# Turning the last batch's x on VectorE and by SBUF transfers, a shorter head sort, and a re-planned order, in an attention and maxout kernel

## The chip, the cores and the metric

The kernel runs on one core of one Trainium2 chip. The metric is the device time of one execution in microseconds. Before the change the median of three runs is 190.68 us (189.26 to 191.23).

## The reference

```python
scores = scale * np.matmul(q, k.transpose(0, 1, 3, 2))      # B 4, H 8, S 768, D 64
stream_keep = causal & (is_sink | in_win)                   # 4 sinks, window 64
mask = np.where(retrieval_head, causal, stream_keep)        # is_retrieval = [1,0,1,0,0,0,1,0]
a = softmax(np.where(mask, scores, -1e9))
x = np.matmul(a, v).transpose(0, 2, 1, 3).reshape(B * S, H * D)
h1, h2 = x @ w1, x @ w2                                      # 512 x 1024 each
out = np.maximum(h1, h2) @ w_out                             # 1024 x 512, float32
```

## The kernel before, in words

**Heads.** Before anything else `head_order` (L1329) reads the eight flags and ranks the heads with ten small VectorE instructions on one partition: three heads with full causal attention ("F") come first, then five streaming heads ("S"), and a count. `values_load_multi_w_load_instructions` (L1413) loads the result into registers of every engine, and a branch (L1419) picks `tile_paired_heads` if the count is three. Only what needs no head number can be issued ahead of the branch: the mask table and two quarters of `moe_w2` (L1407).

**Attention.** A batch is four pairs of heads in the slots FF, FS, SS, SS; pair n of the program is batch n // 4, slot n % 4, so there are 16. A pair's q, k and v are loaded by SP's queue, cast to bf16 (L316, shared by all copies of VectorE and GpSimd; L314 is ScalarE's), and q and k are turned so that the head dimension lies on partitions: for n < 8 on TensorE (`turn`, tile pt, L405) with a copy from PSUM (`unturn`), after that by VectorE's 32x32 squares (`turn_squares`, L418) from a load that already placed the blocks (L349). Then for each tile of up to 8 blocks of 128x128: `scores` (tile ps, L480, with mask products L453 in the first batch), `exp` on ScalarE (tile at, L497), a mask product on VectorE (L519, from the second batch on), `weighted` (tile po, L541), and per half (three blocks of 128 tokens) `normalise` (reciprocal L556, two products L558), which writes the batch's x, 768 tokens x 512 features.

**x turned.** The second stage needs x with features on partitions (tile xt). `turn_x` (tile px, L574) does this on TensorE in 24 transposes of 128x128 a batch, 12 for each half, and `take_x` copies px to xt on VectorE or ScalarE in four copies a batch.

**Maxout.** max(x w1, x w2) w_out is computed as relu(x (w1 - w2)) w_out + x (w2 w_out). `up` (ph, L590) makes one of 8 column blocks for one half (384 tokens) in 4 matmuls, `relu` is on ScalarE (L601) or VectorE (L603), `down` (pout, L617) gives 128 tokens in 12 matmuls of 512 columns, `take_out` copies it and `store` (L655) sends it; the last 128 tokens are split in two column halves (L632, L644). w1 - w2 (`subtract`, L721), the bf16 w2, its turned form (`turn_w2`, pw, L676; `take_w2`) and w2 w_out (`product`, po2, L690) are made during the first batch and the start of the second. w1 and w_out come through the four buffers of q and k loads ("qn"), so their loads wait for casts.

**Order.** Everything after the branch is recorded as operations with a cost, dependences and a rank; `Order.run` (L118) plays it as a schedule with one clock per engine and emits the instructions in that order, so each engine's instruction stream is fixed when the program is built. TensorE takes from lists in the order TX (turn_x), W (weighted), S, TQ, F (up, down), P (weights), and D (`warm`, L729), products nobody reads, at most up to the planned time 20. The outputs of all but the scores share four PSUM banks, given out by the plan. The costs, the time at which the engines begin, and the time until which TensorE is planned at half rate (`order.warm`) are constants in the code.

Of the kernel before, what the change touches and what calls it, by code (L numbers as in the profile page):

```python
# [68 lines left out]
WARM = 60  # L69
# [14 lines left out]
class Order:  # L84
# [6 lines left out]
    def __init__(self, banks):  # L91
        self.ops, self.lists, self.banks = [], {}, banks
        self.users, self.bank, self.queue = [None] * banks, None, None
        self.warm = 0.0
# [23 lines left out]
    def run(self, names, together=(), spare=(), until=0.0, begin=None):  # L118
        free = dict.fromkeys(("PE", "SP", "DMA", "ACT", "DVE", "POOL"), 0.0)
        free.update(begin or {})  # L120
        waiting, pending = [], []
        at = {n: 0 for n in names}
        for k, o in enumerate(self.ops):
            o.number = k
            o.left = sum(d.end is None for d in o.deps) + (o.behind is not None)
            for d in o.deps:
                d.users.append(o)
            if o.behind is not None:
                o.behind.followers.append(o)

# [15 lines left out]
        def free_bank():  # L146

            able = [
                (0.0 if u is None else u.end + u.tail, k)
                for k, u in enumerate(self.users) if u is None or u.end is not None  # L150
            ]
            return min(able) if able else None
# [34 lines left out]
        while True:  # L187
            while waiting and waiting[0][0] <= t:
                pending.append(heapq.heappop(waiting)[2])
            times = [waiting[0][0]] if waiting else []  # L190
            done = False
            for e in ("ACT", "DVE", "POOL", "SP"):
                able = [o for o in pending if e in o.cost or (o.engine == "DMA" and o.by == e)]
                if not able:
                    continue
                if free[e] > t:
                    times.append(free[e])
                    continue
                for o in sorted(able, key=lambda o: (o.rank, o.ready, o.number)):
                    if o.engine == "DMA":  # L200
                        free[e] = t + o.issue
                        start = max(free[e], free["DMA"])
                        free["DMA"] = start + o.cost["DMA"]
                        end = free["DMA"] + 1.6
                    else:
                        end = t + o.cost[e]
                        if any(max(free[x], t) + c < end for x, c in o.cost.items() if x != e):
                            continue
                        free[e] = end
                    pending.remove(o)  # L210
                    o.emit(e)
                    release(o.followers, t)
                    finish(o, end)
                    done = True
                    break
            if free["PE"] <= t:
                best = pick()
                if best and best[1] <= t:
                    n = best[0]
                    now = t  # L220
                    for k in range(2 if n in together and not self.lists[n][at[n]].single else 1):
                        mine = self.lists[n][at[n]:at[n] + 1]
                        w = when(mine[0]) if mine else None
                        if w is None or w > now + 0.3:
                            break
                        o = mine[0]
                        at[n] += 1
                        if o.bank:
                            self.bank = free_bank()[1]
                            self.users[self.bank] = o.bank  # L230
                        o.emit("PE")
                        now += o.cost["PE"] * (2 if now < self.warm else 1)
                        finish(o, now)
                    free["PE"] = now
                    done = True
                elif best:
                    times.append(best[1])
            else:
                times.append(free["PE"])
            if done:  # L240
                continue
            later = [x for x in times if x > t]
            if not later:
                break
            t = min(later)
        for n in spare:
            for o in self.lists.get(n, ())[at[n]:]:
                o.end = t
        left = sum(o.end is None for o in self.ops)
        assert not left, f"{left} operations were not reached"  # L250
        return t


def tile_paired_heads(tc, q, k, v, w1, w2, w2f, wo, out, tab, heads):
# [12 lines left out]
    TURNED, ANY_CASTS = 2 * HP, HP  # L267
# [7 lines left out]
    atp, xp = pool("atp", SLOTS_OF["at"]), pool("xp", SLOTS_OF["x"])  # L275
    gp, small, outp = pool("gp", 2), pool("small", 3), pool("outp", SLOTS_OF["ot"])
# [11 lines left out]
    idle = keep.tile([128, 512], BF16, name="idle")  # L288
    nc.gpsimd.memset(idle, 0.0)
# [286 lines left out]

    def take_x(b, blocks):
        i, m = blocks[0], len(blocks)
        return lambda e: copy(
            e, xts[b % len(xts)][:, i:i + m].rearrange("f i k c -> f i (k c)"), T["px", b, blocks][:, 0:m]  # L580
        )
# [150 lines left out]
    sorted_ = order.given(5.0)  # L732
# [12 lines left out]
    def prepare_w12(half, rank):  # L745
        for two in range(2):
# [7 lines left out]
            for c in range(2):  # L754
                subs[half, two, c] = op(
                    None, {"DVE": 0.68, "POOL": 1.45}, subtract(half, two, c), [o, loaded], rank=rank
                )
                frees.append(subs[half, two, c])

    w2_left = [order.given(3.6 + 1.6 * two) for two in range(2)]  # L760
    for two in range(2):
        prepare_w2(0, two, w2_left[two], -1)

    def prepare_qk(n):
# [24 lines left out]
        if "S" in SLOTS[n % HP]:  # L789
            cost = {"DVE": 0.8 if n < HP else 0.5, "POOL": 1.1}  # L790
# [3 lines left out]
    def prepare_v(n):  # L794
# [6 lines left out]
        if "S" in SLOTS[n % HP]:  # L801
            cost = 0.5 if SLOTS[n % HP] == "FS" else 0.75
# [4 lines left out]
    def attend(n):  # L807
        biased = n < HP
        for t in tiles_of[n]:
# [3 lines left out]
            if biased:  # L813
# [8 lines left out]
                op("DVE", 0.13 + part[1] * part[2] / 1700, mask(n, t, *part), [e], rank=n)  # L822
# [4 lines left out]
        for half in range(2):  # L827
# [3 lines left out]
            norm = op("DVE", 1.0, normalise(n, half), [*done_with["x", b][0]], rank=n)  # L831
# [12 lines left out]
            if p == HP - 1:  # L844
# [13 lines left out]
    for n in range(HP):  # L858
        attend(n)
    prepare_w12(0, HP - 0.7)  # L860
# [61 lines left out]
    for _ in range(WARM):  # L922
        pe("D", 0.43, warm, bank=order.given(0.0))

    order.warm = 8.4
    order.run(
        ("TX", "W", "S", "TQ", "F", "P", "D"), together=("S",), spare=("D",), until=20.0,
        begin={"DMA": 5.8, "SP": 4.6, "DVE": 5.4, "ACT": 4.8, "POOL": 5.0, "PE": 4.7},
# [4 lines left out]
def tile_any_heads(tc, q, k, v, moe_w1, moe_w2, w2f, moe_w_out, out, is_retrieval, n_sink, window):  # L933
# [271 lines left out]

    load_w(moe_w2[:, 512:1024], w2f[:, :, 512:1024])
# [122 lines left out]
def head_order(nc, small, is_retrieval, H):  # L1329


    raw = small.tile([1, 2 * H], I32, name="raw")
# [3 lines left out]
    number = small.tile([1, H], F32, name="number")  # L1336
    for h in range(H):
        nc.vector.memset(number[:, h:h + 1], float(h))
    flag = small.tile([1, 2 * H], F32, name="flag")
    r = small.tile([1, H], F32, name="r1")  # L1340
    key = small.tile([1, H], F32, name="key")
    table = small.tile([1, H, H], F32, name="table")
    rank = small.tile([1, H], F32, name="rank")
# [3 lines left out]
    vec.tensor_single_scalar(out=flag, in_=raw, scalar=0.0, op=ALU.not_equal)  # L1347
    two = flag.rearrange("p (h two) -> p h two", two=2)
    vec.tensor_tensor(out=r, in0=two[:, :, 0], in1=two[:, :, 1], op=ALU.max)
    vec.tensor_reduce(out=found[:, H:H + 1], in_=r, op=ALU.add, axis=AX.X)  # L1350
    vec.scalar_tensor_tensor(
        out=key, in0=r, scalar=-float(H), in1=number, op0=ALU.mult, op1=ALU.add
    )
    by_row = lambda a: a.unsqueeze(2).to_broadcast([1, H, H])
    by_col = lambda a: a.unsqueeze(1).to_broadcast([1, H, H])
    vec.tensor_tensor(out=table, in0=by_col(key), in1=by_row(key), op=ALU.is_lt)
    vec.tensor_reduce(out=rank, in_=table, op=ALU.add, axis=AX.X)
    vec.tensor_tensor(out=table, in0=by_col(rank), in1=by_row(number), op=ALU.is_equal)
    vec.tensor_tensor(out=table, in0=table, in1=by_col(number), op=ALU.mult)
    vec.tensor_reduce(out=found[:, 0:H], in_=table, op=ALU.add, axis=AX.X)  # L1360
    vec.tensor_single_scalar(out=found_i, in_=found, scalar=float(H - 1), op=ALU.min)
# [4 lines left out]
def kernel(  # L1366
# [36 lines left out]

    found = head_order(nc, consts, is_retrieval, H)
    nc.scalar.dma_start(out=tab, in_=table_dram.ap())
    for two in range(2):
        nc.sync.dma_start(  # L1407
            out=w2f[:, 2 * two:2 * two + 2, 0:512],
            in_=moe_w2[256 * two:256 * two + 256, 0:512].rearrange("(c p) f -> p c f", p=128),
        )  # L1410
# [7 lines left out]
    if window <= 64 and n_sink <= 64:  # L1418
        with tc.If(count == N_FULL) as cmp:  # L1419
            tile_paired_heads(tc, *both, tab, heads)  # L1420
# [44 lines left out]
```

## Time and profile before

| | |
|---|---|
| median of three runs | 190.68 us |
| the profiled execution | 190.68 us |
| its span, first to last instruction | 188.6 us |
| outside the span | 2.1 us |
| TensorE busy | 173.3 us, 1706 matmuls |
| VectorE, ScalarE, GpSimd busy | 106.5, 113.7, 61.5 us |
| HBM read, written | 25.43 MB, 6.29 MB |

Times below are counted from the start of the span. A profile gives each instruction's start and duration per engine, and what released it; matmuls overlap in the array, so a group of 128-column transposes that lists 0.5 us each can start one every 56 ns. "Landing" is when a transfer's last packet has arrived and its semaphore says so. An instruction on SP's queue is an issue: it takes a third to half a microsecond there, and the bytes move afterwards on 16 DMA engines.

### The profile page before, as it was taken

To read this page: it belongs to the slowest core of one execution; us is meant where nothing else is said; L and a number is where in the kernel's file an instruction comes from. 1 tells how busy PE (TensorE), PEld (TensorE's weight loads), DVE (VectorE), ACT (ScalarE), POOL (GpSimd) and SP (SyncE) were. 2 spreads that over 40 slices of the span, in tenths; PEclk is the share of its full clock that TensorE was granted. 3 is DMA by queue.
4 is the path that set the end of the run, shared out by engine and by line. 5 is a ranking of instruction groups with operands and counts; after the bars stand their busy time and mean duration, and the time that the engine had idled before them with its cause. 6 is when DMAs were issued, how large, how long until landed. Compare 5 with 4: busy or idle time off the path is not lost.

```text
span 188.6 us, 4670 instructions
## 1 busy us (share of the span) xinstructions
PE 173.3 (92%) x1706; PEld 101.4 (54%) x1706; DVE 106.5 (56%) x249; ACT 113.7 (60%) x167; POOL 61.5 (33%) x82
## 2 busy tenths in 40 slices
PE   0699997999999999999999998899999999999990
PEld 0456654666566556655655465445564545545560
DVE  4547869861599799989998779863740000000000
ACT  3079786778779687747964869275732714625420
POOL 0405496405787345263751526342000000000000
PEclk9999999999999999999999999999999999999998
DMA  5899999899997999999999999833002112012022
GB/s 178 271 303 315 213 287 366 275 299 320 298 286 125 152 153 152 184 169 207 154 200 157 185 191 189 220 150 118 2 30 84 56 57 89 23 59 111 0 107 75
DMA packets 86914, 32.11 MB, mean 170 GB/s; under 512 B 76387, under 2 KB 80739, under 8 KB 86883
## 3 DMA queue, kind: packets, MB, share of 16 engines
q1 hardware_dynamic: 86594, 31.34, 71.3%
q10 hardware_dynamic: 288, 0.39, 0.7%
q8 instruction: 15, 0.25, 0.6%
q14 instruction: 17, 0.13, 0.3%
HBM read 25.43 MB, written 6.29 MB: 168 GB/s over the span
## 4 chain that ended last, share of the span: by engine, by line
PE 74%; DVE 11%; DMA 5%; ACT 3%; issue 2%; POOL 2%; POOLq 1%; ACTq 0%; SPq 0%; DVEq 0%
PE pout L617 28%; PE ph L590 21%; PE po L541 7%; PE ps L480 6%; DVE at L519 5%; DMA w2f<-in_moe_w_dram 4%; PE pt L405 3%; PE po L690 3%; PE px L574 2%; DVE x L558 2%; ACT at L497 2%; PE pout L632 1%; DVE qk L418 1%; PE pw L676 1%; POOL w2b L316 1%
## 5 line engine op out<-in xcount | busy, mean ns | idle before, releaser
L497 ACT ACTIVATE at<-ps 128x1024 bf16<-128x1024 f32 (+3 forms) x68 | 59.4, 917 | 18.4 <-PE ps L480 17.9
L590 PE MATMUL ph<-xt,w 128*128 128x384 bf16 x256 | 44.8, 326 | 1.0 <-DVE g L603 0.8
L617 PE MATMUL pout<-wob,g 128*128 128x512 bf16 x184 | 45.1, 379 | 0.0
L316 POOL CAST qb<-qn 128x768 bf16<-128x768 f32 x26 | 22.8, 880 | 39.4 <-DMA qn<-in_k_dram 20.4
L590 PEld LDWEIGHTS <-w 128*128 128x128 bf16 x256 | 24.1, 98 | 17.3 <-issue 1.0
L601 ACT ACTIVATE g<-ph 128x384 bf16<-128x384 f32 x54 | 26.5, 492 | 9.0 <-PE ph L590 8.8
L519 DVE TENSOR_TENSOR at<-at,tab 128x1024 bf16<-128x1024 bf16 (+5 forms) x45 | 27.8, 644 | 4.6 <-ACT at L497 4.4
L314 ACT COPY ot<-pout 128x512 f32<-128x512 f32 (+1 forms) x22 | 12.7, 577 | 28.2 <-PE pout L617 26.2
L617 PEld LDWEIGHTS <-g 128*128 128x128 bf16 x184 | 16.8, 98 | 18.0
L316 DVE COPY ot<-pout 128x512 f32<-128x512 f32 (+1 forms) x3 | 1.8, 596 | 42.8 <-PE pout L632 42.3
L541 PEld LDWEIGHTS <-at 128*128 128x128 bf16 x472 | 19.8, 98 | 10.9 <-DVE at L519 2.9
L541 PE MATMUL po<-vb,at 128*128 128x65 bf16 x372 | 23.4, 194 | 2.1 <-DVE at L519 1.3
L558 DVE TENSOR_TENSOR x<-po,rez 128x192 f32 x64 | 22.9, 357 | 2.2
L617 PE MATMUL pout<-w2o,xt 128*128 128x512 bf16 x92 | 23.6, 379 | 0.0
L480 PE MATMUL ps<-qk 64*128 64x128 bf16 (+2 forms) x292 | 21.4, 234 | 0.0
L316 POOL CAST vb<-vn 128x768 bf16<-128x768 f32 x16 | 13.6, 850 | 17.1 <-DMA vn<-in_v_dram 14.5
L480 PEld LDWEIGHTS <-qk 64*128 64x128 bf16 x292 | 11.9, 94 | 11.0 <-issue 8.0
L316 POOL COPY vx<-vb 64x650 bf16<-64x650 bf16 (+1 forms) x24 | 17.1, 714 | 1.4
L418 DVE STREAM_TRANSPOSE qk<-qb 128x768 bf16<-128x768 bf16 x16 | 15.4, 965 | 0.0
L617 PEld LDWEIGHTS <-xt 128*128 128x128 bf16 x92 | 8.3, 98 | 8.5 <-issue 0.2
L541 PE MATMUL po<-vx,at 128*128 128x65 bf16 x100 | 10.8, 194 | 0.0
L480 PE MATMUL ps<-qk,kx 64*128 64x128 bf16 x100 | 9.7, 216 | 0.0
(57 smaller groups left out, 139.3 us busy)
## 6 DMA issues: line engine op xcount, KB each, us to landing
vn<-in_v_dram SPq DMA_DIRECT2D x32, 192.0 KB, 4.3
out_dram<-ot SPq DMA_DIRECT2D x23, 256.0 KB, 3.1
qn<-in_q_dram SPq DMA_DIRECT2D x16, 192.0 KB, 4.1
qn<-in_k_dram SPq DMA_DIRECT2D x16, 192.0 KB, 3.9
qn<-in_q_dram SPq DMA_DIRECT2D x32, 96.0 KB, 4.1
qn<-in_k_dram SPq DMA_DIRECT2D x32, 96.0 KB, 3.4
w2f<-in_moe_w_dram SPq DMA_DIRECT2D x4, 512.0 KB, 6.9
w1f<-in_moe_w_dram SPq DMA_DIRECT2D x4, 512.0 KB, 5.9
```

The lines of the kernel that those rows point to most:

```text
L314: nc.scalar.copy(out=out, in_=in_)
L316: eng[e].tensor_copy(out=out, in_=in_)
L405: nc.tensor.transpose(pt[:, i:i + 128], T["qb", n][:, t, i:i + 128], ident)
L418: nc.vector.transpose(T["qk", n][:, t], T["qb", n][:, t])
L480: nc.tensor.matmul(ps[:, bank, e * 128:(e + m) * 128], lhsT=lhsT, rhs=qk[rows, 0, i * 128:(i + m) * 128], start=bank not in begun, stop=Tr ...
L497: nc.scalar.activation(out=at[:, 0:len(w), 0:w[0]], in_=T["ps", n, t][:, 0:len(w), 0:w[0]], func=ACT.Exp, scale=scale,)
L519: eng[e].tensor_tensor(out=at, in0=at, in1=tbl, op=ALU.mult)
L541: nc.tensor.matmul(po[:, hh, b[-1] - 3 * half, :], lhsT=at[:, bank, e * 128:(e + 1) * 128], rhs=rhs, start=first and (bank, hh, e, b) == m ...
L558: nc.vector.tensor_tensor(out=T["x", b][:, 3 * half:3 * half + 3, bass.ds(heads[2 * p + hh], 1), :], in0=po[:, hh, :, 0:D].unsqueeze(2), i ...
L590: nc.tensor.matmul(ph, lhsT=w12[:, kc, fc * 128:(fc + 1) * 128], rhs=xts[b % len(xts)][:, 3 * tg:3 * tg + 3, kc, :], start=(kc == 0), stop ...
L601: nc.scalar.activation(out=g[:, fc, :], in_=ph, func=ACT.Relu)
L617: nc.tensor.matmul(pout, lhsT=lhsT, rhs=rhs, start=(e == 0), stop=(e == len(steps) - 1))
```

## The change

1. `head_order` uses five VectorE instructions in place of ten: a code 2 + h/8 plus the flag, one `max` over the eight codes, which gives them sorted, a sum, and one shift-and-mask that takes head numbers and count out of the float's bits. Within each class the heads now come in falling order.
2. The zero tile `idle` is set before the branch, and six products of it (`FIRST`) run on TensorE ahead of the branch.
3. One quarter of `moe_w2` is loaded ahead of the branch in place of two; the other is loaded after the first batch's q, k and v, and its cast, its turn and the copy of that are planned with a later rank.
4. For the last batch, `turn_x` and `take_x` go. For each half, `turn_x_squares` turns 128 x 1536 elements in 32x32 squares on VectorE into a new tile xs, and 16 transfers from SBUF to SBUF (`regroup_x`, issued by SP, 24 KB each, runs of 64 B) place the squares in xt. They are queued between the stores.
5. Several planned costs, the begin times and `order.warm` are other constants. `vary` adds small random shifts to the ranks of some operations off TensorE, from 24 seeds written in the code. `run` is split into `plan` and emission.

```diff
@@ Order
+    def vary(self, seeds):
+        self.link()
+        movable = [o for o in self.ops if o.engine != "PE"]
+        for seed in seeds:
+            rng = random.Random(seed)
+            for o in rng.sample(movable, rng.choice((1, 2, 4, 8, 20))):
+                o.shift = o.shift + rng.gauss(0, 2.0) if rng.random() < 0.8 else 0.0
...
-                for o in sorted(able, key=lambda o: (o.rank, o.ready, o.number)):
+                for o in sorted(able, key=lambda o: (o.rank + o.shift, o.ready, o.number)):
@@ tile_paired_heads
+    def turn_x_squares(b, half):
+        def emit(_):
+            if half == 0:
+                T["xs", b] = xs_pool.tile([128, NB, d_model], BF16, tag="xs", name="xs")
+            rows = slice(3 * half, 3 * half + 3)
+            nc.vector.transpose(
+                T["xs", b][:, rows].rearrange("p i f -> p (i f)"),
+                T["x", b][:, rows].rearrange("p i h d -> p (i h d)"),
+            )
+        return emit
+    def regroup_x(b, half, g, a):
+        def emit(e):
+            rows = slice(3 * half, 3 * half + 3)
+            src = T["xs", b][32 * g:32 * g + 32, rows].rearrange(
+                "r i (k a s) -> r i k a s", k=KC, a=4
+            )
+            dma[e].dma_start(
+                out=xts[b % len(xts)][32 * a:32 * a + 32, rows, :, 32 * g:32 * g + 32],
+                in_=src[:, :, :, a],
+            )
+        return emit
...
-                    None, {"DVE": 0.68, "POOL": 1.45}, subtract(half, two, c), [o, loaded], rank=rank
+                    None, {"DVE": 0.85, "POOL": 1.3}, subtract(half, two, c), [o, loaded], rank=rank
...
-    w2_left = [order.given(3.6 + 1.6 * two) for two in range(2)]
-    for two in range(2):
-        prepare_w2(0, two, w2_left[two], -1)
+    w2_left = [order.given(4.0)]
+    prepare_w2(0, 0, w2_left[0], -1)
...
-                op("DVE", 0.13 + part[1] * part[2] / 1700, mask(n, t, *part), [e], rank=n)
+                op("DVE", 0.27 + part[1] * part[2] / 1850, mask(n, t, *part), [e], rank=n)
...
-            if p == HP - 1:
+            if p == HP - 1 and b >= SQUARES_FROM:
+                o = op("DVE", 2.0, turn_x_squares(b, half), norms[b, half], rank=n)
+                done_with["x", b][1].append(o)
+                x_ready[b, half] += [
+                    op("DMA", 0.4, regroup_x(b, half, g, a), [o, *done_with["xt", b][0]], rank=n)
+                    for g in range(4) for a in range(4)
+                ]
+            elif p == HP - 1:
...
+    w2_left.append(load(1.6, load_w2(0, 1)))
+    prepare_w2(0, 1, w2_left[1], HP - 0.7)
...
-    order.warm = 8.4
+    order.warm = 7.2
+    order.vary(SEEDS)
     order.run(
...
-        begin={"DMA": 5.8, "SP": 4.6, "DVE": 5.4, "ACT": 4.8, "POOL": 5.0, "PE": 4.7},
+        begin={"DMA": 4.2, "SP": 3.4, "DVE": 4.2, "ACT": 3.6, "POOL": 4.2, "PE": 3.5},
@@ head_order
+        nc.vector.memset(number[:, h], 2 + h / 8)
...
     vec.scalar_tensor_tensor(
+        out=coded, in0=raw.rearrange("p (h two) -> p h two", two=2), scalar=0.0, in1=number,
+        op0=ALU.not_equal, op1=ALU.add,
     )
+    vec.tensor_tensor(out=code, in0=coded[:, :, 0], in1=coded[:, :, 1], op=ALU.max)
+    vec.max(out=found[:, 0:H], in_=code)
+    vec.tensor_reduce(out=found[:, H:H + 1], in_=code, op=ALU.add, axis=AX.X)
+    vec.tensor_scalar(
+        out=found_i, in0=found.bitcast(I32), scalar1=19, scalar2=H - 1,
+        op0=ALU.logical_shift_right, op1=ALU.bitwise_and,
+    )
@@ the kernel, ahead of the branch
     found = head_order(nc, consts, is_retrieval, H)
+    nc.gpsimd.memset(idle, 0.0)
+    with tc.tile_pool(name="first", bufs=1, space=PSUM) as first:
+        unused = first.tile([128, 512], F32, name="unused")
+        for _ in range(FIRST):
+            nc.tensor.matmul(unused, lhsT=idle[:, 0:128], rhs=idle, start=True, stop=True)
     nc.scalar.dma_start(out=tab, in_=table_dram.ap())
-    for two in range(2):
-        nc.sync.dma_start(
-            out=w2f[:, 2 * two:2 * two + 2, 0:512],
...
+    nc.sync.dma_start(
+        out=w2f[:, 0:2, 0:512], in_=moe_w2[0:256, 0:512].rearrange("(c p) f -> p c f", p=128)
+    )
```

## The prediction

> **What bounds the kernel now.** First the page's shares and its slices.
>
> ```profile
> span 188.6 us, 4670 instructions
> PE 173.3 (92%) x1706; PEld 101.4 (54%) x1706; DVE 106.5 (56%) x249; ACT 113.7 (60%) x167; POOL 61.5 (33%) x82
> PE   0699997999999999999999998899999999999990
> DMA  5899999899997999999999999833002112012022
> ```
>
> TensorE is full from about 35 us to 184; the DMA engines are full until about 123. Then the stages (engines in the order PE, PEld, DVE, ACT, POOL; then granted clock, DMA share, GB/s):
>
> ```profile
> 13.00:24.00 11.00, 10.69 (x165) 6.88 (x162) 8.34 (x20) 9.64 (x12) 4.85 (x7) 1.00 1.07 260
> 24.00:35.00 11.00, 9.25 (x145) 5.62 (x143) 8.37 (x23) 8.18 (x12) 8.88 (x10) 1.00 1.00 341
> 47.00:140.00 93.00, 90.68 (x1039) 53.97 (x1038) 76.26 (x171) 63.91 (x89) 42.57 (x53) 1.00 0.90 167
> 140.00:185.00 45.00, 44.30 (x244) 23.40 (x240) 1.11 (x2) 18.78 (x37) 0.00 (x0) 1.00 0.18 68
> ```
>
> From 140 us on TensorE alone works, on maxout that was left over. So a wait in the attention costs only what TensorE then stands idle: what counts is TensorE's work, its gaps, and when its stream begins. Third, the chain of waits (start, length):
>
> ```profile
> 0.76 1.20 DMA raw<-in_is_retrieval_dram
> 1.98 0.17 DVE flag L1347
> ...
> 3.84 0.16 DVE found_i L1361
> 4.04 1.01 POOLq L1413
> ...
> 23.35 8.29 DMA w2f<-in_moe_w_dram
> 31.70 1.05 POOL w2b L316
> 32.79 0.63 PE pw L676 x8
> 33.45 1.01 ACT w2t L314
> 34.46 0.50 ACT xt L314
> 35.00 9.98 PE ph L590 x60
> ...
> 136.93 0.67 PE px L574 x12
> ...
> 139.50 0.67 PE px L574 x12
> ```
>
> The sort is on it, a weight load and the turn of weights are on it just before ph, and both px groups of the last batch. Last, VectorE's casts of the first q and k, which wait for their landing:
>
> ```profile
> 10.26 0.56 DVE L316 CAST qb<-qn 128x768 bf16<-128x768 f32 x1 [0.47 <-DMA qn<-in_k_dram]
> 11.63 0.56 DVE L316 CAST qb<-qn 128x768 bf16<-128x768 f32 x1 [0.82 <-DMA qn<-in_q_dram]
> 12.85 0.56 DVE L316 CAST qb<-qn 128x768 bf16<-128x768 f32 x1 [0.65 <-DMA qn<-in_k_dram]
> ```
>
> **Part 1, the sort.** Ten instructions run from 1.98 to 4.00. Five remain: coded and code take the steps of flag and r (0.19 and 0.20 from start to start), the sum that of L1350 (0.07), found_i 0.16; `max` over eight has no row, between 0.15 (a reduction over eight) and 0.25 (a table step); I take 0.24, nearest to steps that wait for the one before. Sum 0.86 to 0.96, so the result stands 1.1 us earlier, and so do the register loads (1.01 us) and every engine's start: first q issue 5.31 to 4.2.
>
> **Part 2, loads and first tiles.** The trace has the two w2f quarters landing at 5.21 and 7.12, then the first pair's q at 8.63 and 9.14, k at 10.16, and the second pair's k at 12.75: one stream, 0.5 to 0.7 us for 192 KB. With one quarter out of the way (1.9 us) and issues at 4.2, the stream moves by 1.1 (issues only) to 2.2 (issue step 0.52 from a first landing at 6.7, which is 4.2 plus the mask table's 2.7 from issue to landing). On VectorE one cast (0.72) and one copy (0.69) of weights leave the start. I take 1.9: the first scores, at 13.02 now, begin at 11.1.
>
> This stage is paced by ScalarE (9.64 of 11) and by arriving q, k, v, and both move. But the moved quarter now stands between the last v (landing 25.15) and w1f: the w1f quarters, landing at 27.42 and 28.77, come 1.35 (spacing of these two) to 1.9 later in the stream, and so where they were. Their subtractions, three of four now on GpSimd (1.27 each), end near 31.5. The last normalise of batch 0, now to 33.26, moves to 31.4; px and the copy to xt (0.7 each) follow, and the turn of weights that stood on the chain from 31.70 is, in the built order, behind the 64 ph matmuls. So ph begins at 33.1 in place of 35.0; lower bound for this gain 1.2, upper 2.2. The second half of ph needs GpSimd's last subtraction at 38.3; landing near 36 plus 1.27 gives 37.3, so no wait, but a bound of 0.5. Behind ph stands one weight turn more than before (8 matmuls, 0.45), which used to lie under the normalise. Front: 1.9 - 0.45 = **1.45**, between 0.3 and 2.2.
>
> The six early products fill TensorE while it waits for heads; they cost nothing, as 4.0 (start 1.4, six at 0.43) is before the branch at 4.2. They may open the clock earlier: 512 columns took 0.44 at 10.67 and 256 took 0.21 at 13.02, half rate, but 128-column transposes at 14.68 start every 56 ns. The rate changed near 13.5, 7.6 us after the first product at 5.87. The same distance from 1.4 gives 9.0, before the scores; worth 0.3 at most, kept for the range. The Trainium skill ("TensorE: Matmul & The Clock Gate", Part 1) says about 3.4 us of sustained work opens the gate, in a free-running window. By that the dummies alone would open it by 8.2, and the sum would be the same or 0.3 lower; no row here shows a run of 3.4 us without gaps at half rate.
>
> **Part 3, px.** 24 transposes leave TensorE: 0.67 twice in the chain, **1.34**. Four copies leave VectorE and ScalarE (0.69 and 0.59 each half). VectorE gets two turns of 1536 elements; 768 take 0.966 (L418), so 1.93 each. In the built order the first stands ahead of the last normalise and holds one PSUM bank 1.9 us longer, with nothing but pout behind it, which ScalarE copies; no cost.
>
> Cover: in today's times the last po ends at 137.8, the first turn 138.3, the second 141.2. ph of the last batch's first half is 1.34 earlier than now, at 157.0, the second at 170.0. SP's queue, in order, has after the batch's first store (140.2) four transfers, a store (142.8), three, a store (145.4), fourteen, a store, three, a store, four, a store, four; each waits for the one eight issues earlier too. At 0.52 from issue to issue (k loads: 0.32 at least, and 0.19 between) the sixteenth goes at 150.1, and with the loads' median landing (3.8) is there by 153.9: 3.1 before its use. The last goes at 160.3, lands at 164.1: 5.9 before. TensorE does pout and ph of the batch before meanwhile. Stores are behind transfers by up to 7.3 us; four ot buffers, one taken every 2.6 us or less often, cover it. Rows used:
>
> ```profile
> L349 SPq DMA_DIRECT2D qn<-in_k_dram x32: 316/380/1377, 59.0 to 117.0; - x32
> DMA to landing us min/median/max: 2.8/3.8/6.1
> ```
>
> **Part 4, the order.** TensorE's gaps over 0.15 us beyond its matmuls, from starts in the trace, sum to 3.9 us between 47 and 125, the longest at 117.3 (0.98), 116.4 (0.60), 99.0 (0.51), 106.9 (0.49), each behind VectorE or ScalarE. A plan whose mask cost is nearer to the row (1024 columns: 0.82 planned against 0.73 before; rows 0.64 to 1.15) puts more between exp and po. The random ranks may help or not; loads of the second batch come no earlier while TensorE does. Gain bounded by 3.9 above and, as the stage 13 to 35 shows what a worse order costs (3.4 of such gaps), by about -2 below. I take **0.9**, a quarter of what is there.
>
> **Sum.** 188.6 - 1.45 - 1.34 - 0.9 = 184.9 of span, plus 2.1 outside (190.68 - 188.6; this run is the median): **187.0 us**. The end, copy, issue and landing after 184.3, is untouched.
>
> **Rivals.** (A) The load stream takes the front back. For: DMA share 1.00 to 1.07 there, and no byte is saved; idle DMA before 4.2 is lost. Against: ph waited on the weight turn, not on w1f. Then 1.34 and 0.3 stay: 189.0. (B) Slower: the 32 transfers are late and TensorE stands before the last batch's ph. It decides from 0.77 us a transfer for the second half (145.4 + 25p + 1.6 for three stores + 3.8 > 170.0) and 0.86 for the first (145.4 + 9p + 3.8 > 157.0). At the longest k issue, 1.4 us, the second half lands at 185.8 against 170.0: 16 us, 203. For: such issues exist, and runs are 64 B where the loads have 128. Against: they occurred at DMA shares above 1; here it is 0.18, and 12,288 packets at the loads' median 13 ns make 10 us of 16 engines in 20. The Trainium skill ("DMA: Bandwidth & Descriptors", Rules for kernel authors) speaks against the change: transfers under 64 KB are mostly overhead, to be coalesced; with its fixed 2.0 us each, one at a time, my estimate is 64 us for 32. The landing row against it: issues 0.52 apart with 3.8 to land overlap, about seven in flight. (C) The new order has more gaps: +3 in place of -0.9 gives 190.9. For: the stage is near VectorE's limit (76 of 93) and the plan does not know port or DMA contention. (D) The gaps go altogether: 184.0. (E) The sort's integers pick the other branch: with flags 3 of 8 the sum is 22.5 and its bits give 6, which is what the branch compares with; out.
>
> **Chances.** Forecast 0.67; A 0.11; B 0.06; C 0.09; D 0.07. Range of the forecast's own terms: front 0.3 to 2.2 and order -0.3 to 2.0 not all at once, 185.3 to 188.4; with A, 185.2 to 189.2 leaves out B, C, D and a little. One per cent (188.8 and 192.6) is what a measurement here tells from none. Faster: forecast, D, and a third of A, 0.78; same: rest of A, most of C, 0.15; slower 0.07.
>
> **What would show it.** found_i ending near 2.9 and the first q issue near 4.2; first scores near 11.1; ph from 33.1 with no gap inside; L574 with 72 matmuls; transfers 0.5 apart with no TensorE idle before the last two ph groups; gaps from 47 to 140 near 3 us. Wrong if ph still begins near 35, if SP's issues near the end are over 0.77 apart, or if TensorE waits for VectorE in batches 1 to 3 grow.

## The result and the profile after

The kernel after the change takes 186.83 us in the median of six runs (186.25 to 188.43), the kernel before, on the same chip, 190.03 us (189.25 to 191.23). The ratio is 0.9863, with an interval of 0.9818 to 0.9907: faster by 0.9 to 1.8%; the quotient of the two medians, 0.983, lies inside that interval. Ratios leave out runs more than 1.5% above the fastest run of their kernel, while medians and ranges hold all runs. The profiled execution of after is its shortest run, 186.25 us, with a span of 184.4 us and so 1.85 us outside it.

The page's shares and slices of after:

```profile
span 184.4 us, 4648 instructions
PE 170.2 (92%) x1667; PEld 98.7 (54%) x1689; DVE 106.8 (58%) x232; ACT 112.2 (61%) x166; POOL 66.5 (36%) x93
PE   6678987999999899998999999999999999999990
DMA  5899899989999799999999899422014434533032
```

TensorE now has something to do in the first slices (the six early products), and the DMA engines, at 0 to 0.2 there before, are at 0.3 to 0.5 in slices 31 to 37 (138 to 171 us): the 32 transfers lie in it. The trace lacks 22 of the 1689 matmul records, so starts are compared below and not busy sums. The same by stage (stretch, its length, busy time and count of PE, PEld, DVE, ACT, POOL, then granted clock, DMA share, GB/s):

```profile
13.00:24.00 11.00, 9.98 (x164) 6.82 (x165) 9.23 (x22) 9.60 (x13) 6.67 (x10) 1.00 0.99 277
24.00:35.00 11.00, 9.12 (x132) 5.90 (x133) 10.02 (x23) 7.80 (x10) 9.63 (x9) 1.00 1.01 368
47.00:140.00 93.00, 90.61 (x1014) 53.30 (x1027) 76.52 (x159) 64.43 (x89) 44.32 (x62) 1.00 0.77 165
140.00:181.00 41.00, 39.96 (x219) 21.47 (x220) 0.42 (x1) 17.43 (x34) 0.00 (x0) 1.00 0.36 87
```

From 140 us on TensorE still works alone, now with transfers on the DMA engines beside it. The chain of waits of after (start, length), at the places that were shown of before:

```profile
0.76 1.20 DMA raw<-in_is_retrieval_dram
2.06 0.17 DVE coded L1416
...
2.70 0.16 DVE found_i L1423
2.89 0.95 SPq L1483
...
6.80 3.78 DMA qn<-in_q_dram
10.60 0.57 DVE qb L346
...
30.69 0.37 DVE x L588
31.09 0.37 DVE x L588
31.50 0.86 PE px L604 x12
32.39 0.84 PE px L604 x12
33.23 10.40 PE ph L646 x64
```

The head result stands at 2.86 us, not 4.00. The weight load of 8.29 us and the turn of weights are gone from the place ahead of ph; there stand the last normalise of the first batch and its px, and ph follows at 33.1 to 33.2 (35.0 before). No px group of the last batch is left. VectorE's casts of the first q and k:

```profile
9.01 0.56 DVE L346 CAST qb<-qn 128x768 bf16<-128x768 f32 x1 [0.96 <-DMA qn<-in_k_dram]
10.60 0.56 DVE L346 CAST qb<-qn 128x768 bf16<-128x768 f32 x1 [1.04 <-DMA qn<-in_q_dram]
11.80 0.56 DVE L346 CAST qb<-qn 128x768 bf16<-128x768 f32 x1 [0.64 <-DMA qn<-in_k_dram]
```

They begin 1.25, 1.03 and 1.05 us earlier than before. The first of the four, at 9.23 before, gained most (7.49, so 1.74): what the moved quarter gave the first load was used up two loads later, and 1.05 is about the 1.1 of the sort.

The last new thing is the line of the transfers (issue time min, median, max in ns, first and last start), and the line of the two turns on VectorE:

```profile
L627 SPq DMA_DIRECT2D xt<-xs x32: 586/618/1096, 137.1 to 161.6; - x32
L614 DVE STREAM_TRANSPOSE xs<-x x2: 1772/1776/1779, 135.3 to 138.0; 128x1536 bf16<-128x1536 bf16 x2
...
DMA to landing us min/median/max: 1.9/2.0/3.0
```

The last transfer goes at 161.6 and has landed at 163.56; the ph that needs it begins at 167.12. The first half's last one (in the order as built it is the seventeenth of the 32) has landed at 151.71, its ph begins at 154.15. TensorE waits for neither: in the chain of after each of these ph groups follows the pout before it without a gap.

```profile
146.65 7.50 PE pout L673 x34
154.15 5.20 PE ph L646 x32
...
159.62 7.50 PE pout L673 x34
167.12 5.20 PE ph L646 x32
```

**Where the time went.** From the starts of TensorE's stages, before and after (us). "Work" is the sum of its matmuls at their distance at full rate, "gaps" is the rest. (A 128-column transpose of px lists 0.22 us, and not the 0.5 given above, and starts 56 ns after the one before it; the distance is what counts.)

| | before | after | change |
|---|---|---|---|
| first scores | 13.02 | 11.56 | -1.46 |
| ph of batch 0 | 35.00 | 33.08 | -1.92 |
| first po2 | 46.58 | 44.70 | -1.88 |
| last po | 137.58 | 135.80 | -1.78 |
| last matmul begins | 184.02 | 179.84 | -4.18 |
| work, first scores to the end | 165.70 | 164.80 | -0.90 |
| gaps, first scores to ph | 4.26 | 3.80 | -0.46 |
| gaps, ph to last po | 1.03 | -0.32 | -1.35 |

The group that ends with the last matmul, in the chain of before and in that of after:

```profile
181.68 2.63 PE pout L632 x24
```

```profile
177.50 2.63 PE pout L688 x24
```

So 4.18 = 1.46 (start) + 0.90 (work) + 1.81 (gaps), and work is 1.34 of transposes removed less 0.45 for a turn of weights that came to lie behind the first scores. (The negative gap is an error of the work figure, which counts some paired score matmuls too high, in both kernels alike; only differences are used.) The table compares the two profiled runs, which are 4.43 us apart (190.68 and 186.25), where the medians are 3.20 apart. It says where that pair differs, and is not to be read as an exact account of the medians.

### The profile page after: what moved, and what is told of

The parts are those of the page before. It is cut to its first block, busy times and chain, and to the rows that moved or that the text cites. A ratio compares the mean times of both kernels' runs of the same rounds, so it can differ in the third digit from the quotient of the medians.

```text
span 184.4 us, 4648 instructions
## 1 busy us (share of the span) xinstructions
PE 170.2 (92%) x1667; PEld 98.7 (54%) x1689; DVE 106.8 (58%) x232; ACT 112.2 (61%) x166; POOL 66.5 (36%) x93
## 4 chain that ended last, share of the span: by engine, by line
PE 80%; DVE 7%; ACT 4%; DMA 3%; issue 2%; SPq 2%; ACTq 0%; DVEq 0%
PE pout L673 30%; PE ph L646 22%; PE ps L510 8%; PE po L571 8%; PE po L746 3%; ACT at L527 3%; DVE at L549 3%; PE pt L435 2%; PE px L604 2%; DMA qn<-in_q_dram 2%; DVE x L588 2%; PE pout L688 1%; SPq L373 1%; ACT qk L344 1%; PE ps L483 1%
## 5 line engine op out<-in xcount | busy, mean ns | idle before, releaser
L673 PE MATMUL pout<-wob,g 128*128 128x512 bf16 x179 | 43.6, 379 | 0.5 <-issue 0.3
L657 ACT ACTIVATE g<-ph 128x384 bf16<-128x384 f32 x58 | 28.5, 491 | 10.2 <-PE ph L646 9.8
L571 PEld LDWEIGHTS <-at 128*128 128x128 bf16 x472 | 19.3, 97 | 9.7 <-DVE at L549 1.4
L571 PE MATMUL po<-vb,at 128*128 128x65 bf16 x372 | 22.5, 194 | 1.7 <-ACT at L527 0.9
L673 PE MATMUL pout<-w2o,xt 128*128 128x512 bf16 x82 | 22.5, 379 | 0.9 <-DVE x L588 0.2
L346 POOL CAST vb<-vn 128x768 bf16<-128x768 f32 x16 | 13.5, 843 | 15.5 <-DMA vn<-in_v_dram 14.3
L346 POOL COPY kx<-qk 128x320 bf16<-128x320 bf16 (+1 forms) x12 | 5.1, 456 | 20.2 <-DVE qk L448 18.1
L344 ACT COPY qk<-pt 128x768 bf16<-128x768 bf16 x9 | 7.2, 800 | 8.3 <-PE pt L435 8.2
```

The costliest lines, as they stand in the source:

```text
L344: nc.scalar.copy(out=out, in_=in_)
L346: eng[e].tensor_copy(out=out, in_=in_)
L571: nc.tensor.matmul(po[:, hh, b[-1] - 3 * half, :], lhsT=at[:, bank, e * 128:(e + 1) * 128], rhs=rhs, start=first and (bank, hh, e, b) == m ...
L657: nc.scalar.activation(out=g[:, fc, :], in_=ph, func=ACT.Relu)
L673: nc.tensor.matmul(pout, lhsT=lhsT, rhs=rhs, start=(e == 0), stop=(e == len(steps) - 1))
```

## The experiments

Theory: three separate gains add up, the sort at the start, the transposes that left TensorE, and a better planned order; the transfers are covered by slack. Rivals: the random shifts, not the costs, give the order's gain; the moved quarter gives the start; TensorE's clock gives or takes part of it; and rival B of the prediction, that late transfers can undo it all. Each ratio is against runs of the kernel before made beside it; the kernels were run in three groups, and the median of before was 191.36, 190.03 and 191.42 us in them.

### The sort alone, and the squares alone

The kernel before with the new sort, its order as it was:

```diff
@@ before, head_order and the branch
-    vec.tensor_single_scalar(out=flag, in_=raw, scalar=0.0, op=ALU.not_equal)
...
+    vec.max(out=found[:, 0:H], in_=code)
...
-    with tc.If(count == N_FULL) as cmp:
+    with tc.If(count == (N_FULL + 3) % H) as cmp:
```

> The kernel before with the five-instruction sort alone; every engine's order stays that of before. If the start passes through to the end: first q issue at 4.2 in place of 5.31, ph (L590) from about 34.0 in place of 35.0, time 0.8 to 1.1 us below before. If the load stream takes the front back: ph at 35.0, time within 0.3 us of before.

Measured: 188.35 us (186.76 to 190.53), ratio 0.9871 (0.9799 to 0.9944). In its trace, of a run of 189.94 us and so among its longer ones, the first q goes at 4.16, the first scores begin 0.81 earlier than before, ph 0.75, the last po 1.13 and the last matmul 1.13. So the sort carries the start: 1.1 us at the issues, 0.75 to 0.81 in the first stages, and 1.13 again at the last matmul. What follows the last matmul varies: here it takes 5.28 us against 4.53, so this run's span is only 0.39 shorter than that of before (188.17 against 188.55). The ratio gives more than the expected 0.8 to 1.1 us, 1.1 to 3.8 us by its interval.

The kernel before with squares and transfers for the last batch, and nothing else:

```diff
@@ before
+            if p == HP - 1 and b >= SQUARES_FROM:
+                o = op("DVE", 2.0, turn_x_squares(b, half), norms[b, half], rank=n)
...
+                    op("DMA", 0.4, regroup_x(b, half, g, a), [o, *done_with["xt", b][0]], rank=n)
...
-            if p == HP - 1:
+            elif p == HP - 1:
```

> The kernel before with the last batch's x turned by VectorE and 32 transfers, nothing else (costs, begin times, no shifts as before). If the term for px is right: 24 matmuls fewer, 1.3 us below before, no idle TensorE ahead of the last two groups of ph, transfers 0.5 to 0.7 us apart. If the transfers are late: an idle TensorE before them and a time above that of before.

Measured: 188.5 us (187.56 to 190.94), ratio 0.989 (0.9817 to 0.9963). Work falls by 1.34 (165.70 to 164.36); gaps fall by 0.90 more, with the first scores 0.16 later. TensorE waits for no transfer here either: they go from 137.4 to 163.3. So the transposes are worth what they cost, and the old plan's gaps moved a little by themselves. The two parts' last matmuls come 1.13 and 2.08 earlier; 0.97 of the 4.18 is left for the moved quarter, the early products and the new order. That holds between single profiled runs. By the ratios, the two parts alone (0.9871 and 0.989) would give 2.4% together, more than the 1.4% of the whole change (0.9863); the intervals are too wide to tell whether the parts add up, and that they do is not shown.

### The order: shifts or costs, and the clock

```diff
-    order.vary(SEEDS)
+    order.vary(())
```

> The changed kernel without the random rank shifts, all else kept (planned costs and begin times too). If the shifts carry the order's gain: the stretch from the first product of weights (po2) to the last po is about 1.3 us longer than in the changed kernel, time about 188. If the measured costs carry it: within 0.4 us of the changed kernel, 186.8.

Measured: 188.51 us (185.92 to 189.26), ratio 0.984 (0.9751 to 0.9929); the profiled run is 188.84, near the top of that range. From the first po2 to the last po its gaps are -0.01, near those of after, while its ph begins at 34.53, 1.45 later than after's. The windows of this run say why (columns as above):

```profile
1.21:4.62 3.41, 3.12 (x7) 0.86 (x8) 1.05 (x8) 1.40 (x2) 0.38 (x5) 1.00 0.64 228
4.62:8.03 3.41, 1.53 (x14) 0.66 (x13) 2.18 (x5) 0.00 (x0) 0.00 (x0) 1.00 0.78 210
8.03:11.45 3.42, 2.64 (x17) 1.48 (x18) 1.12 (x2) 1.54 (x2) 0.00 (x0) 0.50 0.96 299
11.45:14.86 3.41, 3.41 (x30) 1.88 (x29) 0.56 (x1) 2.45 (x4) 0.83 (x1) 0.50 1.11 315
```

The stretches are cut where the granted clock changed. The view shows 1.00 ahead of the first change too, where nothing is on record; the six early products there start every 0.42 us, where 512 columns at full rate take 0.22: half rate. The clock opened at 4.62, after a stretch with TensorE busy 3.12 of 3.41 us; closed at 8.03, after one with 1.53; stayed closed after one with 2.64; and opened again at 14.86. In the profiled run of after:

```profile
3.34:6.75 3.41, 2.93 (x13) 1.12 (x12) 1.40 (x4) 0.00 (x0) 0.32 (x4) 1.00 0.64 215
6.75:10.16 3.41, 1.69 (x16) 0.79 (x14) 1.71 (x3) 0.80 (x1) 0.00 (x0) 1.00 0.96 279
```

it opened at 6.75 and stayed open through a stretch with 1.69. Part of what the shifts seemed to give may therefore be the clock. To take it out, `warm` was made to issue two products where it issued one:

```diff
@@ warm
-        nc.tensor.matmul(px, lhsT=ident, rhs=idle, start=True, stop=True)
+        for _ in range(2):
+            nc.tensor.matmul(px, lhsT=ident, rhs=idle, start=True, stop=True)
```

once on after, and once without the shifts, beside after itself:

> The changed kernel once more, beside the next three. Between 186 and 188.5 us, as its first six runs; if the clock's state in the first 15 us divides the runs, they fall near 186.3 where it stays open and near 188 where it closes again.

> The changed kernel with two products that nobody reads in place of one, at each of the same places, before about 16 us. The order of everything else is the same. If the clock closes again in runs where TensorE is idle more than half of a window while q and k land: now it stays open, no run above 187.3, median 186.2 or lower. If the spread has another cause: spread and median as the changed kernel's, or 0.2 us more for the added products.

> No random shifts of ranks, and twice the unread products. Without shifts the runs fell into 186.0 (two) and 188.4 to 189.3 (four), and the profiled one shows the clock closed from 8.0 to 14.9. If that is the clock: all runs near 186.0, and so the shifts are worth 0.3 us or less. If the shifts mend the order: still 188 and above.

| | median us (range) | ratio (interval) | clock opens | ph | last matmul |
|---|---|---|---|---|---|
| after again | 186.89 (186.35 to 189.21) | 0.9854 (0.9797 to 0.9911) | 9.39 | 33.55 | 180.13 |
| after, two products | 185.97 (184.39 to 186.88) | 0.9796 (0.9735 to 0.9857) | 5.36 | 32.35 | 179.79 |
| no shifts, two products | 186.62 (185.73 to 188.04) | 0.9849 (0.9786 to 0.9911) | 4.24 | 32.85 | 179.94 |

The runs of the repeat do not divide by the clock in the way that was expected of them. One with a mean granted clock of 0.982 took 186.46 us, one with 1.0 took 189.21; that mean counts the time before the first change on record as full rate, so it does not tell when the clock opened. The two dense kernels were expected to keep all runs up to 187.3, and all near 186.0; the first did (186.88 at most), the second did not (187.4 and 188.04).

In the profiled runs of these two dense kernels the clock stays open once it has opened, until the work ends. Without the shifts, but with the open clock, the last matmul comes within 0.15 us of the same kernel with them, and the gaps from po2 to the last po are -0.58 against -0.21. So the shifts are not what closed the gaps of batches 1 to 3; the new costs are, or the rest of the new plan, which were not tried apart. In one profiled run against another the last matmul comes 2.46 us earlier with two products (182.40 to 179.94). Of this, 1.68 is there at ph already (34.53 to 32.85), behind the stretch in which the clock had closed; the other 0.78 arose later, with the clock open in both. The one without was among the longer runs of its kernel (188.84), and the ratios of the two, which stand on different chips, do not separate (0.984 and 0.9849). So what the clock costs in a typical run is not shown. After with two products is the fastest version seen, but its interval overlaps that of after.

The six early products were taken away from after:

```diff
-    with tc.tile_pool(name="first", bufs=1, space=PSUM) as first:
-        unused = first.tile([128, 512], F32, name="unused")
-        for _ in range(FIRST):
-            nc.tensor.matmul(unused, lhsT=idle[:, 0:128], rhs=idle, start=True, stop=True)
```

> The changed kernel without the six products ahead of the branch. If they cost and bring nothing (prediction's sum): within 0.3 us of the changed kernel. If the early clock is worth something: the clock opens a window or two of 3.4 us later (near 10 to 13.5) and the time is 0.5 to 1.5 us longer.

Measured: 187.08 us (186.23 to 188.39), ratio 0.9864 (0.9812 to 0.9916), against 0.9854 with them: no difference that these runs can tell. Its profiled run, the longest of the six at 188.39 us, shows the clock opening as late as 15.74, beyond the 10 to 13.5 expected, and ph at 34.33. The early products are not shown to be worth anything.

### The moved quarter

No shifts, but both quarters ahead of the branch again; then the same with two products in `warm`:

```diff
+    for two in range(2):
         nc.sync.dma_start(
-            out=w2f[:, 0:2, 0:512],
+            out=w2f[:, 2 * two:2 * two + 2, 0:512],
...
-    w2_left.append(load(1.6, load_w2(0, 1)))
-    prepare_w2(0, 1, w2_left[1], HP - 0.7)
```

> As the one without shifts, but both quarters of w2 loaded ahead of the branch again and both turned early. If leaving one quarter for later moved the first scores: they begin 0.4 to 0.8 us later than without shifts, and the time is 0 to 0.8 us longer, since 8 matmuls (0.45 us) go back to the start where TensorE waits. If it is only a matter of where the bytes stand in one stream: same time within 0.3 us.

> No shifts, twice the unread products, both quarters of w2 loaded ahead of the branch. If the moved quarter is worth its place: first scores 0.6 to 1.3 us later than with one quarter (11.5) and the time above 186.6. If only the clock held the earlier pair apart: first scores later but ph as early or earlier, since the load stream behind the heads is 1.4 us shorter, and the time 186.6 or less.

Measured: 187.53 us (187.27 to 187.81), ratio 0.9857 (0.98 to 0.9913), and with two products 186.89 (185.67 to 188.54), ratio 0.9801 (0.9736 to 0.9866). With both quarters first, the first scores come 1.3 us later than in the kernel without shifts (13.08 against 11.77), more than the 0.4 to 0.8 expected, so the quarter does move the first scores; but ph comes 0.4 earlier (34.13 against 34.53) and the end 1.56 earlier (180.84 against 182.40). With two products the first scores come 2.8 later and the end 2.3 later (182.24 against 179.94), in a run (188.54 us, the longest of its six) whose clock closed from 9.89 to 13.30 all the same, so two products do not always hold it open. In the first of the two kernels the clock was closed from 7.67 to 14.50, and yet its six runs lie between 187.27 and 187.81, with mean granted clocks from 0.979 to 0.995. The ratios, 0.9857 and 0.9801 with both quarters first, 0.984 and 0.9849 without, overlap. The worth of the moved quarter at the end stays open: it is not shown to be anything.

### What the transfers hang on

Each transfer of after cut in three, one for each block of 128 tokens, the order otherwise as it was:

```diff
@@ regroup_x
+            for i in range(3):
                 dma[e].dma_start(
-                    out=xts[b % len(xts)][32 * a:32 * a + 32, rows, :, 32 * g:32 * g + 32],
-                    in_=src[:, :, :, a],
+                    out=xts[b % len(xts)][32 * a:32 * a + 32, 3 * half + i, :, 32 * g:32 * g + 32],
+                    in_=src[:, i, :, a],
                 )
```

> The changed kernel with each of the 32 transfers cut in three, of a third of the runs each, at the same places of SP's queue. If an issue costs what a load's does whatever it holds (0.52 to 0.66 apart): 64 more issues, the first half lands near 165 where its ph would begin near 154, and the second near 192; the time is 20 to 30 us above the changed kernel. If an issue's time goes with its runs (a third of 0.66, 0.22): the 96 take as long as the 32, and the time is the changed kernel's within 0.5 us.

Measured: 227.6 us (226.88 to 228.32), ratio 1.1951 (1.1836 to 1.2067). Its transfers and the wait that they cause (us in total, times, the longest):

```profile
L628 SPq DMA_DIRECT2D xt<-xs x96: 585/599/1953, 136.9 to 203.2; - x96
```

```profile
PE ph L647 <- DMA xt<-xs: 35.5, 2, 20.4
```

A third of the bytes takes about as long to issue (599 against 618 ns): the price is by the piece. TensorE stands before both ph groups for 35.5 us, and its clock is at half rate from 159.28 to 179.76 and from 193.41 to 210.48, which makes the gaps after the last po 41.1 in all. The time is about 40 us above the changed kernel's, where 20 to 30 were expected. This is rival B, priced: 32 issues are under its point, 96 far beyond.

Other seeds, in the version with two products:

```diff
-SEEDS = (
...
-)
+SEEDS = tuple(range(1, 25))
```

> As the changed kernel with twice the unread products, but the 24 seeds are 1 to 24. If the seeds that were kept are a better order than chance: slower than with them (186.0) by 1 us or more, the gaps in front of ph or between po2 and the last po longer. If the order is robust and the planned costs carry it: within 0.6 us of the two with twice the unread products, 186.0 and 186.6.

Measured: 198.09 us (196.96 to 200.05), ratio 1.0396 (1.0325 to 1.0466). Up to the last po, at 134.96, it is no later than after. Then:

```profile
PE ph L643 <- DMA xt<-xs: 7.3, 1, 7.3
```

and in the chain of waits (start, length)

```profile
160.95 1.94 DMA xt<-xs
162.90 0.27 issue
163.17 7.29 PE ph L643 x32
```

Its transfers are not slower (0.66 us apart, the first at 135.7 and the last at 160.95, where after has 137.1 and 161.6), and the ph of the first half could begin at 155.9. But the shifts changed their order: as built, the last of the 32 is one of the first half's, which is the seventeenth in after and the sixteenth without shifts. So TensorE waited for the whole queue, 7.3 us, and then worked at half rate until 167.12. Rival B happened, by the place of one transfer and not by the price of it.

The last two batches by squares, without shifts, with two products:

```diff
-    TURNED, ANY_CASTS, SQUARES_FROM = 2 * HP, HP, B - 1
+    TURNED, ANY_CASTS, SQUARES_FROM = 2 * HP, HP, B - 2
```

> As the one without shifts and with twice the unread products, but x of the last two batches is turned by VectorE and transfers. If TensorE's work alone counts: 24 matmuls fewer, 1.3 us below 186.6. If SP's queue is the limit: the plan gives a transfer 0.55 us of SP, the changed kernel's trace shows 0.66 from issue to issue, so 32 of them are 3.5 us later than planned; TensorE stands before the third batch's ph and the time is 1 to 4 us above 186.6.

Measured: 192.97 us (192.04 to 194.21), ratio 1.0129 (1.0064 to 1.0193). Its waits of TensorE:

```profile
PE po L571 <- DVE at L549: 3.5, 4, 1.9
...
PE ps L510 <- ACT at L527: 1.7, 3, 0.9
```

and, in the answer for the line of its transfers, who else waited for them:

```profile
  DVE xs L614: 6.2, 1
```

Another 24 transposes leave TensorE (work 163.68 against 165.02 in the same kernel with one batch), but the gaps from po2 to the last po grow to 5.64, from -0.58, and those behind it to 1.69. In the kernel with one batch, the third batch's ph begins at 126.0 and fills TensorE among the last batch's scores and po: from 104 to 134 us it is busy 29.96 of 30 us. Here that ph needs transfers, the first of which goes at 115.94, behind the last loads of v and two stores on SP's queue, and it begins only at 133.0. Between 122 and 133 TensorE stands before scores for exp and before po for masks (the two lines above; with one batch, 0.8 us of waits for masks in the whole run). After two stretches in which TensorE was so little busy, the clock closed (columns as above):

```profile
120.44:123.85 3.41, 2.00 (x37) 1.38 (x36) 2.40 (x7) 2.66 (x4) 0.75 (x2) 1.00 0.29 34
...
130.68:134.09 3.41, 1.54 (x31) 1.19 (x28) 3.06 (x9) 1.58 (x3) 0.00 (x0) 1.00 0.35 39
```

It was closed from 123.85 to 127.26 and from 134.09 to 137.50, about 1.7 us lost each time. The 6.2 us are VectorE's own wait, since the only xs buffer was still being read by transfers; it lies behind the last po (135.75 to 141.95), and TensorE shows no wait that comes from it. So TensorE did not stand before ph itself, as the second expectation had it: the late ph left it without work beside the attention. That this is the reason is read from the two traces and was not tried apart; the two turns, 1.75 us each, also stand on VectorE at 105.81. Its last matmul comes 6.94 us later than with one batch (186.88 against 179.94), and by the two ratios, 1.0129 and 0.9849, the loss is 2.8%, 5.3 us, more than the 1 to 4 expected. With a second xs buffer, or the transfers ahead of other issues, it was not tried.

## Why the prediction was right

The forecast was 187.0 us with 185.2 to 189.2; the median is 186.83. That the two numbers are so close is in part luck. From the 190.68 at which it started, the forecast was a gain of 3.68 us (1.9%); the ratio gives 0.9 to 1.8%, the medians 3.20 us, since before took 190.03 beside after, and the profiled pair 4.43 us. Its own steps:

- **Sort (part 1): right.** First q issue at 4.17 against 4.2, found_i done at 2.86 against 2.9. `max` took 0.08 from start to start (2.45 to 2.53), not 0.24; it was below the nearest row.
- **Front (part 2): the sum right, its parts less so, and so partly luck.** ph at 33.1 as forecast, behind the normalise (to 31.46, forecast 31.4) and px as the text had it, and the first scores with the added turn gave 1.46 and 0.46 of gaps less 0.45 of work: 1.47 against 1.45. But the 1.9 for the stream was 1.46 at the first scores, and at the fourth cast only 1.05, the lower bound that the text called "issues only". The missing part came back as fewer gaps between first scores and ph. The moved quarter does bring the first scores 1.3 us earlier where it was tried alone, but ph and the end did not follow it there.
- **Clock ("worth 0.3 at most"): too small in one pair of profiles, its size open.** The opening near 9.0 was 6.75 in the profiled run and 9.39 in the repeat. What the text did not see is that the clock can close again before it holds; in the pair of profiled runs that showed this, ph moved by 1.68 us, but the ratios do not separate the two kernels. The six early products alone fill only about 2.5 us (from 1.33); the stretch ahead of the opening at 6.75 had 2.93 of 3.41 with turns of weights and unread products among them. The Trainium skill ("TensorE: Matmul & The Clock Gate", Part 1) has a free-running window of about 3.4 us, and the trace agrees: changes lie 3.4 us, or a multiple of it, apart. Its idle window is not what closed the clock here: the stretch before 8.03 in the kernel without shifts had TensorE busy 1.53 of 3.41 us, and its longest gap was 1.02 us.
- **px (part 3): right.** 1.34 of work, alone and in the whole. The turn on VectorE took 1.78 against 1.93.
- **Transfers: cover right, sizes off both ways.** 0.66 us from one to the next against 0.52, 2.0 to land against 3.8. They overlap: all 32 went and landed in 26.4 us (137.14 to 163.56), not in the 64 of one at a time. The last one of the first half is the seventeenth of the queue as built, and not the sixteenth. The slack was 2.4 us for the first half (3.1 forecast) and 3.6 for the second (5.9 forecast), so the shorter landing made up for part of the longer step. The step that was measured, 0.66, stands nearer to the tipping points of 0.86 and 0.77 us a transfer than the 0.52 that was taken.
- **Order (part 4): right in sign, 1.35 against 0.9** from ph to the last po. The 0.9 was a share of the gaps, chosen without a row that gives it, so its size is a lucky guess; and that the new mask cost closed the gaps was not tried apart. The text left open whether the random ranks help; with the clock held open they give nothing that these runs can tell, and other seeds cost 11 us (1.0396 against 0.9796).
- **Rivals.** A fell (ph did begin at 33.1), C fell (the gaps shrank), D would have needed all 3.9 us. B did not happen in this kernel and is real in two neighbours, by more pieces and by the place of one piece in the queue. E fell.

Against the profiled run the span is 184.4 where the sum gave 184.9, nearly all of the difference from the order; outside the span it is 1.85 where 2.1 was kept unchanged, a 0.25 that the sum did not have.

## What to carry to other kernels

Small transfers on SP's in-order queue were priced by the piece (0.60 us to issue 8 KB, 0.62 for 24 KB), and whoever needs a group of them waits for the one that stands last: count the pieces, take the issue step from a row of the same kind, and look at the place of the last one of each group in the built order. Work moved off TensorE gained 1.34 us in the last batch, where slack covered the transfers, and cost 5 to 7 us when the batch before was moved too, where the ph that had filled TensorE beside the attention came later. Before an order is believed to be better, see when the granted clock opened in its profile and whether it closed again.

## What was not expected of the hardware

The granted clock changes only at steps of about 3.41 us, and needs little idle time to close. In the fourteen profiled runs a stretch before an opening had TensorE busy 2.77 to 3.41 of 3.41 us; stretches with 2.64, 2.76, 2.81 and 2.84 did not open it. Stretches with 1.53, 1.19 and 1.12 closed it, and 1.69 (after) and 1.81 (no shifts, two products) kept it open, though 2.00 and 1.54 closed it in the kernel with two batches by squares. The busy time of these stretches is modelled and the ranges overlap, so no sharp edge follows from them. Filling that opens the clock need not hold it: without shifts, a stretch with 3.12 opened it and the next, with 1.53, closed it. Part of that may be that the same matmuls take less time once the clock is open; it was not tried apart.

An issue of an SBUF to SBUF transfer on SP's queue took a median of 0.62 us for 24 KB and 0.60 us for 8 KB, where a load of k took 0.38 in the kernel before.
